# Casting the next chunk's B and C one part a step, behind a bank copy on ScalarE

## The chip, the cores and the metric

The kernel runs on one core of a Trainium2 chip. The metric is the device time of one launch in microseconds, as the median of several runs. The engines of the core are TensorE (PE, with its weight loads as PEld), VectorE (DVE), ScalarE (ACT), GpSimd (POOL) and SyncE (SP). Here SP computes nothing; it only issues the DMAs, all on one queue.

## What is computed

Three layers follow one another. The first is a linear attention (a scan with decay) over 4 batches, 8 heads and 768 positions, with head dimension 32 and state size 16. The second and third are feed-forward layers on the 3072 x 256 result. The reference computes the scan in chunks; this is the core of it:

```python
for c in range(nc):
    CB = np.einsum('bhin,bhjn->bhij', Cc, Bc)
    M = CB * L                                  # L: decay from j to i, causal
    y_intra = np.einsum('bhij,bhjd->bhid', M, xc)
    y_inter = np.einsum('bhin,bhnd->bhid', Cc, state) * decay_to_i[:, :, :, None]
    y[:, :, sl] = y_intra + y_inter
    state = decay_full * state + np.sum(Bx, axis=2)
h = np.maximum(np.maximum(x @ w1, x @ w2), x @ w3)      # layer 1, d_ff 768
x = h @ w_out
gate = 1.0 / (1.0 + np.exp(-(x @ w_gate)))              # layer 2, d_ff 1536
out = gate * (x @ w_val) @ w_out
```

## The kernel before, in words

**Attention.** The kernel cuts the 768 positions into 8 chunks of 96 (`CH`), and each chunk into 8 steps of four of the 32 (batch, head) units, so there are 64 steps. A step (`attention`, L259) computes the scores of its four units on PE (L273, from `bi` and `cs`, into the PSUM tile `s`), multiplies them by decays into `mt`, and multiplies `xs` by `mt` into the PSUM tile `y` (L291). Steps with an even number copy the scores on ACT (L281) and multiply on POOL (L282); the others do both at once on DVE (L285). After every four steps the result goes to `xt_hi` (ACT, L300) and `xt_lo` (DVE, L302), the input of layer 1.

**B and C.** From chunk 2 on, the scores need B and C as three bfloat16 parts each. `split_bc` (L231) does this for one chunk. It loads the 128 x 896 tile `bc`, then three times casts it on ACT into one third of the tile `parts` (L239) and copies that third with DMAs into `bi` and `cs` (L244); between two casts POOL subtracts the part from `bc` (L248). The first cast is followed by six copies, the second by four, the third by two. The tiles `bc` and `parts` exist once. `bi` exists twice (even and odd chunks), and so does `cs`. The generator of chunk c+1 is put into the list `pipe` by `prepare` (L311) at the first step of chunk c. Every tick of the program then takes each generator in `pipe` one stage further, however many steps are begun between two ticks. `prepare` also loads the decays of four pairs of steps ahead (`load_decay`, L206, four buffers) and scans those that have come (L228, on DVE).

**Feed-forward layers.** Layer 1 has six tiles of 512 tokens (`t`) and six blocks of 128 hidden columns (`m`); its banks are called u3_t_m_j, for j from 0 to 2. `layer` computes the three up-projections of a block into three PSUM banks. The pool of these banks, `psu`, has three buffers, and the scores tiles `s` come out of the same pool. Fp32 products are made of three matmuls of split operands (L338 to L340). `most` (L380) copies the first bank into `s3_t_m` on ACT (L383, the bank copy), takes the maximum with the other two on DVE (L385, L387), and `hidden` splits the result into `hi` (ACT, L376) and `lo` (POOL, L378), which the down-projection reads (o6 in the order, `o` in the trace). The attention of later chunks is woven into layer 1, and from token tile 2 on its steps are begun two at a time. Layer 2 begins once layer 1 is through; its weights are loaded and decoded before, when attention has ended and its memory is free.

**Order of the work.** The program's order, the pools and the waits go through a scheduler that places every instruction at a simulated time, and from that comes one fixed order for each engine. On the chip each engine works through that order and waits where a semaphore isn't there yet. `tc.issue_after(i)` adds an edge without a semaphore: what is written inside the block on the engine of `i` comes behind `i` in that engine's order.

Of the kernel before, what the change touches and what calls it, by code (L numbers as in the profile page):

```python
# [66 lines left out]
def scan_attention_then_ffn(ctx: ExitStack, tc: tile.TileContext, xh, ah, bch, pick, bn, w1, w2, w3,  # L67
                            wo1, wg, wv, wo2, out):
    nc = tc.nc
    act, dve, pool, pe, sp = nc.scalar, nc.vector, nc.gpsimd, nc.tensor, nc.sync  # L70
# [13 lines left out]
    pipe = Pipe()  # L84
# [119 lines left out]
    def load_decay(n, src):  # L204
        t = awk.tile([128, PU, LW], F32, tag="dec", bufs=DECS, name=f"dec{n}")
        i = sp.dma_start(out=t.rearrange("p u w -> p (u w)"), in_=src[n].partition_broadcast(128))  # L206
        dec[n] = t
        for _ in range(BEHIND.get(n, 0)):
            with tc.issue_after(i.ins):
                load_weights()  # L210

    def load_x(c, part=slice(0, NU)):
        if c not in xs:
            xs[c] = awk.tile([128, NU, D], F32, tag="xs", name=f"xs{c}")
            bx[c] = awk.tile([128, NU, N], F32, tag="bx", name=f"bx{c}")
        for t, src, n in ((xs[c], xh, D), (bx[c], bn, N)):
            sp.dma_start(out=t[:, part].rearrange("i u d -> i (u d)"),
                         in_=src[:, c, n * part.start:n * part.stop])

    def decay(n, clip=False):  # L220

        t = dec[n]
        if clip:
            dve.tensor_scalar(out=t[:, :, 1:LW], in0=t[:, :, 1:LW], scalar1=1e-6, scalar2=1.0,
                              op0=ALU.max, op1=ALU.min)
        for h in range(PU // 4):
            f = t[:, 4 * h:4 * h + 4].rearrange("p u w -> p (u w)")
            dve.tensor_tensor_scan(out=f, data0=f, data1=delta.rearrange("p u w -> p (u w)"),  # L228
                                   initial=0.0, op0=ALU.mult, op1=ALU.add)

    def split_bc(c):  # L231

        r = awk.tile([128, BW + 384], F32, tag="bc", bufs=1, name=f"bc{c}")
        sp.dma_start(out=r, in_=bch[:, c])
        parts = awk.tile([128, 3, BW + 384], BF16, tag="parts", bufs=1, name=f"parts{c}")
        cs[c] = awk.tile([KT, NU, CH], BF16, tag="cs", name=f"cs{c}")
        yield
        for p in range(3):
            act.copy(parts[:, p], r)  # L239
            for k, (dst, cols) in enumerate(((bi[c % 2], slice(0, BW)),  # L240
                                             (cs[c], slice(BW, BW + 384)))):
                for t, pr in enumerate(TERMS):
                    if pr[k] == p:
                        sp.dma_start(  # L244
                            out=dst[16 * t:16 * t + 16].rearrange("n (g q) i -> n g (q i)", q=4),
                            in_=parts[:, p, cols])
            if p < 2:
                pool.tensor_tensor(out=r, in0=r, in1=parts[:, p], op=ALU.subtract)  # L248
                yield

    steps = [(c, g) for c in range(NC) for g in range(NG)]
    done = [0]
    last = [None]

    def need(t):
# [3 lines left out]
    def attention(k, ahead):  # L259
# [24 lines left out]
        else:  # L284
            last[0] = dve.tensor_tensor(out=m[:, :, 0:CH], in0=ps[:, :, 0:CH], in1=dc[:, :, 1:LW],  # L285
                                        op=ALU.mult)
        prepare(k)
        yield
        y = ys[g // 4]
# [21 lines left out]
    def prepare(k):  # L311

        c, g = divmod(k, NG)
        if g == 0 and 0 < c < NC - 1:
            load_x(c + 1)
            pipe.add(split_bc(c + 1))
        n = k // 2
        if k % 2 == 0:
            if 5 <= n + 4 < NC * NP:
                load_decay(n + 4, ad)  # L320
        elif k < 9:
            decay(n + 1, n == 0)
        else:
            for i in ([n + 1] if k == 9 else []) + [n + 2]:
                if i < NC * NP:
                    with tc.issue_after(last[0].ins) if k > FIRST else ExitStack():
                        decay(i)
# [46 lines left out]
    def hidden(s, hl, eng):  # L374
        yield
        act.copy(hl[0], s)  # L376
        yield
        eng.tensor_tensor(out=hl[1], in0=s, in1=hl[0].bitcast(F32), op=ALU.subtract)  # L378

    def most(s, banks, hl):  # L380

        yield
        act.copy(s, banks[0])  # L383
        yield
        dve.tensor_tensor(out=s, in0=banks[1], in1=s, op=ALU.max)  # L385
        yield
        dve.tensor_tensor(out=s, in0=banks[2], in1=s, op=ALU.max)  # L387
        yield from hidden(s, hl, pool)
# [73 lines left out]
    for t in range(NTT):  # L462
        for m in range(M1):
            for hl in layer(t, m, wt1[m], 3, most):
                slot_end()
                slot += 1
            if pend is not None:
                down(*pend)
            slot_end()
            slot += 1  # L470
            pend = (t, m, M1, wt1[m], hl, finish1)
            if t == NTT - 1 and m == 0:
                actx.close()
                wp2.append(ctx.enter_context(tc.tile_pool(name="wp2", bufs=1)))
                todo += [(piece2, m, part) for m in range(M2) for part in range(2)]
                while todo:
                    load_weights()
            if t == NTT - 1 and m == 3:
                pipe.add(split_y(0))
# [84 lines left out]
```

## Time and profile before

| what | us |
|---|---|
| runs of the kernel before | 606.14, 601.85, 602.65 |
| median | 602.65 |
| the profiled execution | 604.28 |
| its span, first to last instruction | 602.5 |
| PE busy in it | 563.0 |
| mean granted clock of PE | 0.974 |

The profile is one execution. Times in its rows are microseconds from the start of the span unless they are marked ns. A row of instructions names the engine, the line, the operation, and the tiles as out<-in. In square brackets stands how long the engine was idle before the instruction and what ended that idle time. SPq is the DMA queue of SP. A matmul's row can overlap the next one, since matmuls are pipelined. Trace rows leave the buffer and step numbers out of tile names; the order of the instructions has them.

### The profile page before, as it was taken

The numbers are of one execution on the slowest core, as the hardware profiler recorded it, in microseconds if no ns is written. First come the engines' busy times: TensorE is split into PE (matmuls) and PEld (weight loads), VectorE is DVE, ScalarE is ACT, GpSimd is POOL, SyncE is SP. The second block draws the span as 40 slices with busy tenths as digits, with TensorE's granted clock in tenths as the row PEclk, the third lists the DMA queues.
The fourth block names the chain that finished last, engine by engine and source line by source line (L and its number), as shares of the span: only waits on it lengthen the run. The fifth ranks groups of instructions, "written<-read, shape, count | busy, mean of one in ns | idle before, by whom it ended". The sixth has DMA issues, their size and how long they took to land.

```text
span 602.5 us, 8006 instructions
## 1 busy us (share of the span) xinstructions
PE 563.0 (93%) x2992; PEld 444.7 (74%) x2992; DVE 317.5 (53%) x467; ACT 260.0 (43%) x475; POOL 186.0 (31%) x207
## 2 busy tenths in 40 slices
PE   5778797997989999999999999999999999999997
PEld 4656575675767777777768888888888888888885
DVE  4899962644745755368987133344344334334332
ACT  5777653224233223279897243233233223223322
POOL 3668874335453424237668210000000000000000
PEclk9859998998999989999999999999999999999999
DMA  7998975373763900099000000000000000000000
GB/s 252 326 313 233 205 183 93 102 132 86 155 134 83 178 28 1 1 316 312 1 2 0 2 35 1 0 1 35 2 0 36 0 1 36 1 1 35 1 0 35
DMA packets 35367, 50.53 MB, mean 84 GB/s; under 512 B 3456, under 2 KB 24320, under 8 KB 35328
## 3 DMA queue, kind: packets, MB, share of 16 engines
q1 hardware_dynamic: 35328, 50.02, 32.0%
q8 instruction: 23, 0.38, 0.3%
q14 instruction: 16, 0.13, 0.1%
HBM read 38.51 MB, written 3.25 MB: 69 GB/s over the span
## 4 chain that ended last, share of the span: by engine, by line
PE 63%; DVE 9%; DMA 8%; ACT 5%; issue 4%; POOL 2%; SPq 1%; DVEq 0%; ACTq 0%; POOLq 0%
PE u L338 14%; PE u L339 14%; PE u L340 14%; PE o L339 7%; PE o L340 6%; PE o L338 6%; DMA cs<-parts 4%; DVE dec L228 2%; DMA dec<-ad 1%; DMA bc<-in_bch 1%; DVE t_b L142 1%; DVE s L387 1%; DVE s L385 1%; PE y L291 1%; POOL lo L378 1%
## 5 line engine op out<-in xcount | busy, mean ns | idle before, releaser
L376 ACT CAST hi<-s 128x512 fp32r<-128x512 f32 x108 | 67.1, 621 | 193.1 <-DVE s L394 153.8
L394 DVE TENSOR_TENSOR s<-u,s 128x512 f32<-128x512 f32 x72 | 49.7, 690 | 126.2 <-PE u L340 125.9
L338 PE MATMUL u<-xt_hi,w_b 128*128 128x512 f32 x288 | 112.4, 390 | 0.8 <-DVE s L385 0.6
L339 PE MATMUL u<-xt_lo,w_b 128*128 128x512 f32 x288 | 112.1, 389 | 0.0
L340 PE MATMUL u<-xt_hi,w_b 128*128 128x512 f32 x288 | 112.1, 389 | 0.0
L338 PE MATMUL u<-xt_hi,w_a 128*128 128x512 f32 x216 | 90.8, 420 | 10.4 <-ACT s L383 5.8
L339 PE MATMUL u<-xt_lo,w_a 128*128 128x512 f32 x216 | 87.2, 404 | 1.8 <-DVE xt_lo L302 1.8
L340 PE MATMUL u<-xt_hi,w_a 128*128 128x512 f32 x216 | 87.0, 403 | 0.0
L378 POOL TENSOR_TENSOR lo<-s,hi 128x512 fp32r<-128x512 f32 x48 | 66.4, 1384 | 64.1 <-ACT hi L376 63.0
L338 PEld LDWEIGHTS u<-xt_hi,w_b 128*128 128x128 f32 x288 | 54.1, 188 | 13.3 <-DVE s L385 1.1
L378 DVE TENSOR_TENSOR lo<-s,hi 128x512 fp32r<-128x512 f32 x60 | 41.5, 692 | 40.6 <-ACT hi L376 40.4
L340 PEld LDWEIGHTS u<-xt_hi,w_b 128*128 128x128 f32 x288 | 54.1, 188 | 11.3
L339 PEld LDWEIGHTS u<-xt_lo,w_b 128*128 128x128 f32 x288 | 54.1, 188 | 11.0
L338 PEld LDWEIGHTS u<-xt_hi,w_a 128*128 128x128 f32 x216 | 42.2, 195 | 25.1 <-ACT s L383 8.0
L228 DVE TENSOR_TENSOR_SCAN dec<-dec,delta 128x388 f32<-128x388 f32 x64 | 57.9, 944 | 3.2 <-DMA dec<-ad 3.0
L339 PE MATMUL o<-lo,w_b 128*128 128x512 f32 x144 | 56.1, 390 | 0.0
L340 PE MATMUL o<-hi,w_b 128*128 128x512 f32 x144 | 56.0, 389 | 0.0
L339 PEld LDWEIGHTS u<-xt_lo,w_a 128*128 128x128 f32 x216 | 42.1, 195 | 10.3 <-DVE xt_lo L302 2.3
L340 PEld LDWEIGHTS u<-xt_hi,w_a 128*128 128x128 f32 x216 | 42.0, 194 | 9.5
L392 ACT ACTIVATE s<-u 128x512 f32<-128x512 f32 x72 | 43.2, 600 | 10.8 <-PE u L340 9.8
L385 DVE TENSOR_TENSOR s<-u,s 128x512 f32<-128x512 f32 x36 | 24.6, 685 | 40.4 <-PE u L340 25.8
L338 PE MATMUL o<-hi,w_b 128*128 128x512 f32 x144 | 45.3, 390 | 0.5 <-ACT hi L376 0.5
(60 smaller groups left out, 761.6 us busy)
## 6 DMA issues: line engine op xcount, KB each, us to landing
dec<-ad SPq DMA_DIRECT2D x30, 388.0 KB, 5.6
raw_a<-in_w SPq DMA_DIRECT2D x18, 256.0 KB, 6.2
bi<-parts SPq DMA_DIRECT2D x36, 128.0 KB, 6.7
cs<-parts SPq DMA_DIRECT2D x36, 96.0 KB, 6.8
xs<-in_xh SPq DMA_DIRECT2D x6, 512.0 KB, 7.1
raw_b<-in_wg SPq DMA_DIRECT2D x12, 256.0 KB, 5.8
raw_b<-in_wv SPq DMA_DIRECT2D x12, 256.0 KB, 5.8
raw_b<-in_wo SPq DMA_DIRECT2D x12, 256.0 KB, 5.8
```

What stands on the lines that cost most here:

```text
L142: dve.scalar_tensor_tensor(out=t, in0=f1, scalar=3, in1=sg, op0=ALU.logical_shift_left, op1=ALU.bitwise_or)
L228: dve.tensor_tensor_scan(out=f, data0=f, data1=delta.rearrange("p u w -> p (u w)"), initial=0.0, op0=ALU.mult, op1=ALU.add)
L291: pe.matmul(y[32 * q:32 * q + 32, g % 4, 0:CH + N], xs[c][:, 4 * g + q, :], m[:, q, :], start=True, stop=True)
L338: pe.matmul(ps, wlo, a_hi(k), start=k == 0, stop=False)
L339: pe.matmul(ps, whi, a_lo(k), start=False, stop=False)
L340: pe.matmul(ps, whi, a_hi(k), start=False, stop=k == kn - 1)
L376: act.copy(hl[0], s)
L378: eng.tensor_tensor(out=hl[1], in0=s, in1=hl[0].bitcast(F32), op=ALU.subtract)
L385: dve.tensor_tensor(out=s, in0=banks[1], in1=s, op=ALU.max)
L387: dve.tensor_tensor(out=s, in0=banks[2], in1=s, op=ALU.max)
L392: act.activation(out=s, in_=banks[0], func=AF.Sigmoid)
L394: dve.tensor_tensor(out=s, in0=banks[1], in1=s, op=ALU.mult)
```

## The change

The generator of the next chunk is kept in a list `splits` and no longer in `pipe`. `prepare`, which runs once for each of the 64 steps, takes it one stage further, so the load is issued at the first step of a chunk, and the three casts come at the second, third and fourth. From chunk 3 on each cast is also written behind the last bank copy of `most` traced so far (`evict[0]`). The generator yields `splits` itself after its third cast, and so `prepare` knows that it has ended.

```diff
@@ split_bc
         for p in range(3):
-            act.copy(parts[:, p], r)
+            with tc.issue_after(evict[0].ins) if c > 2 else ExitStack():
+                act.copy(parts[:, p], r)
...
             if p < 2:
                 pool.tensor_tensor(out=r, in0=r, in1=parts[:, p], op=ALU.subtract)
-                yield
+            yield splits if p == 2 else None
@@
     done = [0]
+    evict = [None]
+    splits = []
@@ prepare
             load_x(c + 1)
-            pipe.add(split_bc(c + 1))
+            splits.append(split_bc(c + 1))
+        if splits and next(splits[0], None) is splits:
+            splits.pop()
@@ most
-        act.copy(s, banks[0])
+        evict[0] = act.copy(s, banks[0])
```

Line numbers after the change are higher: L239 becomes L240, L244 becomes L245, L281 becomes L284, L376 becomes L381, L383 becomes L388.

The first place is ScalarE's order at the first two blocks of token tile 1 in layer 1, before. In `s3_1_0` stand the number of banks, the token tile and the block; `parts5` is chunk 5's; the last number of a name is a running one.

```order
L383 COPY s3_1_0_951<-u3_1_0_0_954 128x512
L281 COPY mt4_102<-s3_0_962 128x4x96
L239 CAST parts5_1378<-bc5_1376 128x896
L357 COPY y1_91<-o6_0_0_640 128x512
L376 CAST hi3_1_0_952<-s3_1_0_951 128x512
L357 COPY y1_91<-o6_0_1_641 128x512
L239 CAST parts5_1378<-bc5_1376 128x896
L383 COPY s3_1_1_1025<-u3_1_1_0_1028 128x512
L281 COPY mt1_99<-s3_2_1048 128x4x96
```

The same place in ScalarE's order after the change:

```order
L388 COPY s3_1_0_951<-u3_1_0_0_954 128x512
L240 CAST parts4_985<-bc4_983 128x896
L284 COPY mt4_102<-s3_0_962 128x4x96
L362 COPY y1_91<-o6_0_0_640 128x512
L362 COPY y1_91<-o6_0_1_641 128x512
L381 CAST hi3_1_0_952<-s3_1_0_951 128x512
L388 COPY s3_1_1_1025<-u3_1_1_0_1028 128x512
L240 CAST parts4_985<-bc4_983 128x896
L284 COPY mt1_99<-s3_2_1042 128x4x96
```

Chunk 5's casts have left this place and chunk 4's stand here, each directly behind a bank copy; before, chunk 4's stood ahead of these rows.

The second place is ScalarE's order at blocks 3 and 4 of token tile 2, before:

```order
L383 COPY s3_2_3_1550<-u3_2_3_0_1553 128x512
L281 COPY mt0_98<-s5_0_1569 128x4x96
L300 CAST xt_hi_92<-y1_104 128x2x2x96
L281 COPY mt2_100<-s5_2_1634 128x4x96
L376 CAST hi3_2_3_1551<-s3_2_3_1550 128x512
L239 CAST parts7_1941<-bc7_1939 128x896
L383 COPY s3_2_4_1644<-u3_2_4_0_1647 128x512
L239 CAST parts7_1941<-bc7_1939 128x896
```

The same place in ScalarE's order after the change:

```order
L388 COPY s3_2_3_1550<-u3_2_3_0_1553 128x512
L240 CAST parts6_1611<-bc6_1609 128x896
L284 COPY mt0_98<-s5_0_1569 128x4x96
L303 CAST xt_hi_92<-y1_104 128x2x2x96
L284 COPY mt2_100<-s5_2_1642 128x4x96
L381 CAST hi3_2_3_1551<-s3_2_3_1550 128x512
L388 COPY s3_2_4_1652<-u3_2_4_0_1655 128x512
L240 CAST parts6_1611<-bc6_1609 128x896
```

Where a cast of chunk 7 stood ahead of the bank copy of block 4, a cast of chunk 6 now stands behind that copy, and another behind the bank copy of block 3. Chunk 7's stand in token tile 3.

The third place is SyncE's queue where chunk 7's copies are issued, before. `dec28` is the decay load of steps 56 and 57.

```order
L206 DMA dec27_1851<-ad_105 128x776
L244 DMA bi1_97<-parts7_1941 16x8x512
L244 DMA cs7_1942<-parts7_1941 16x8x384 x3
L244 DMA bi1_97<-parts7_1941 16x8x512
L217 DMA xs7_1912<-in_xh 128x1024
L244 DMA bi1_97<-parts7_1941 16x8x512
L244 DMA cs7_1942<-parts7_1941 16x8x384 x2
L206 DMA dec28_1916<-ad_105 128x776
```

The same place in SyncE's queue after the change:

```order
L206 DMA dec27_1851<-ad_105 128x776
L245 DMA bi1_97<-parts7_1918 16x8x512 x3
L245 DMA cs7_1919<-parts7_1918 16x8x384
L217 DMA xs7_1912<-in_xh 128x1024
L245 DMA cs7_1919<-parts7_1918 16x8x384 x2
L206 DMA dec28_1920<-ad_105 128x776
```

Before, two more copies into `bi1` stand ahead of `dec27`, so `dec28` had ten copies of chunk 7 ahead of it; now it has the six of the first cast, and the four of the second come behind it.

## Rows read from the trace of the kernel before

**Rows 1.** Page, part 1: busy time, share of the span, instructions.
```profile
PE 563.0 (93%) x2992; PEld 444.7 (74%) x2992; DVE 317.5 (53%) x467; ACT 260.0 (43%) x475; POOL 186.0 (31%) x207
```

**Rows 2.** Busy time by stretches: length, PE PEld DVE ACT POOL, PE clock, DMA share, GB/s.
```profile
97.80:100.27 2.47, 0.00 (x0) 0.00 (x1) 0.00 (x0) 1.99 (x4) 0.92 (x1) 0.99 0.02 6
100.27:102.76 2.49, 1.28 (x2) 0.57 (x2) 0.00 (x0) 1.93 (x4) 2.49 (x4) 0.50 0.00 0
102.76:107.20 4.44, 4.44 (x12) 3.20 (x13) 0.69 (x1) 1.25 (x2) 2.96 (x3) 0.52 0.11 15
...
136.96:140.77 3.81, 0.00 (x1) 0.00 (x0) 0.86 (x2) 1.47 (x3) 0.46 (x1) 1.00 0.13 26
140.77:145.30 4.53, 4.53 (x14) 3.39 (x15) 0.69 (x1) 2.25 (x4) 4.44 (x4) 0.62 0.28 69
...
167.10:186.00 18.90, 15.76 (x85) 11.58 (x85) 8.81 (x16) 7.05 (x12) 9.99 (x11) 1.00 0.44 84
...
209.90:212.47 2.57, 0.87 (x21) 0.57 (x20) 2.39 (x7) 0.48 (x1) 1.18 (x2) 1.00 0.04 12
212.47:216.00 3.53, 3.53 (x9) 2.84 (x10) 2.13 (x3) 1.21 (x2) 1.53 (x2) 0.55 0.37 113
```

**Rows 3.** Waits of PE, 75 to 255 us: total us, times, longest.
```profile
PE u L338 <- ACT s L383: 5.3, 2, 3.8
PE o L338 <- ACT hi L376: 2.5, 1, 2.5
PE o L339 <- POOL lo L378: 2.5, 3, 1.2
PE s L273 <- DVE s L385: 1.2, 1, 1.2
PE u L338 <- DVE s L387: 0.9, 2, 0.5
```

**Rows 4.** Timeline of ACT: start, duration, instruction, idle time before it.
```profile
98.28 0.94 ACT L239 CAST parts<-bc 128x896 bf16<-128x896 f32 x1 [9.06 <-DMA bc<-in_bch]
...
139.30 0.94 ACT L239 CAST parts<-bc 128x896 bf16<-128x896 f32 x1 [5.43 <-DMA cs<-parts]
140.14 0.58 ACT L383 COPY s<-u 128x512 f32<-128x512 f32 x1
...
174.07 0.94 ACT L239 CAST parts<-bc 128x896 bf16<-128x896 f32 x1 [5.85 <-DMA cs<-parts]
```

**Rows 5.** Instructions on the tile parts: ns min/median/max; last, its copies' time to landing.
```profile
L244 SPq DMA_DIRECT2D cs<-parts x36: 547/597/1571, 26.7 to 200.6; - x36
L239 ACT CAST parts<-bc x18: 921/938/942, 19.1 to 180.0; 128x896 bf16<-128x896 f32 x18
L248 POOL TENSOR_TENSOR bc<-bc,parts x12: 1887/1900/2351, 20.1 to 178.0; 128x896 f32<-128x896 f32 x12
...
DMA to landing us min/median/max: 3.0/6.7/9.4
```

**Rows 6.** Line 234, the load of bc: time from issue to landing.
```profile
DMA to landing us min/median/max: 3.3/5.1/7.4
```

**Rows 7.** Timeline of all engines, 147.8 to 161.2 us.
```profile
147.86 0.59 ACT L383 COPY s<-u 128x512 f32<-128x512 f32 x1 [0.20 <-PE u L340]
...
151.05 0.69 DVE L387 TENSOR_TENSOR s<-u,s 128x512 f32<-128x512 f32 x1 [1.02 <-PE u L340]
...
151.78 0.33 SPq L217 DMA_DIRECT2D bx<-in_bn  x1
...
159.22 0.53 SPq L206 DMA_DIRECT2D dec<-ad  x1
...
160.81 0.34 PE L273 MATMUL s<-cs,bi 96*128 96x96 bf16 x4
161.01 0.59 ACT L383 COPY s<-u 128x512 f32<-128x512 f32 x1
```

**Rows 8.** Timeline of DVE at 207 us.
```profile
207.44 1.81 DVE L228 TENSOR_TENSOR_SCAN dec<-dec,delta 128x388 f32<-128x388 f32 x2 [1.22 <-DMA dec<-ad]
```

## The prediction

> **What bounds the kernel now.** I read the page's busy table first, then busy time by stretches, then the list of waits of TensorE (PE), then the timelines of the engines at its stops. PE is busy 93% of the span and no other engine reaches 60% [rows 1], so an edit on ScalarE (ACT) counts only where it lets PE stop, or where it takes such a stop away. The stretches show where PE stops between 75 and 255 us [rows 2]. It is idle for 2.47 us from 97.80, for 1.21 of the next 2.49 (busy 1.28), for 3.81 from 136.96, for 3.14 of the 18.90 from 167.10 (busy 15.76), and for 1.70 of the 2.57 from 209.90 (busy 0.87). That is 12.3 us, and the list of waits adds up to the same: 5.3 + 2.5 + 2.5 + 1.2 + 0.9 = 12.4 [rows 3].
>
> After three of these stops the matmuls also run slower. The granted clock is 0.50 and 0.52 behind the first stop, 0.62 behind the second and 0.55 behind the last; 0.50 is the 1.2 GHz level, and before each fall PE had stood still. In the stretch from 167.10, with several shorter stops, it stays at 1.00, the 2.4 GHz level [rows 2]. A busy stretch of length L at a mean clock c loses about (1 - c) x L: 0.50 x 1.28 = 0.64, 0.48 x 4.44 = 2.13, 0.38 x 4.53 = 1.72, 0.45 x 3.53 = 1.59. Idle and clock together are 18.4 us, all that can be won here.
>
> Who holds PE up? In the first three stops an instruction of ACT: its copy of a bank (L383), which frees PSUM for PE, or the cast hi (L376), which the down-projection reads [rows 3]. ACT's own timeline shows what it was doing: it sat 9.06 us before the cast at 98.28, waiting for the load bc, 5.43 before the one at 139.30 and 5.85 before the one at 174.07, both waiting for copies out of parts [rows 4]. The bank copy at 140.14 follows directly on the second [rows 4]. These are first casts of chunks 5, 6 and 7. ACT works in order, so a cast that waits for a DMA holds every bank copy behind it.
>
> **The change part by part.** Same instructions, other places: 18 casts of 0.94 us, 12 subtractions of 1.90 us on GpSimd (POOL), 72 copies on SP's queue [rows 5]. Nothing is added or removed. ScalarE's order shows the move: chunk 5's casts leave the first blocks of tile 1, chunk 4's stand there, each directly behind a bank copy, and where chunk 7's casts stood now stand chunk 6's. The casts come up to a chunk later, so their inputs have long landed.
>
> *First stop.* The 9.06 us wait goes. Chunk 4's casts, now in its place, need a load that landed long before and are separated by the subtraction of 1.90 us [rows 5], which runs while PE works on the next bank. Won: 2.47 + 1.21 + 0.64 + 2.13 = 6.45.
>
> *Second stop.* The bank copy comes before the cast instead of behind it. Won: 3.81 + 1.72 = 5.53.
>
> *Third stop.* 3.14, less 0.45 that is one of the two waits for DVE L387 [rows 3], which the casts don't cause: 2.69, no clock lost.
>
> *Last stop.* 1.24 of the 1.70 is the wait s L273 <- DVE s L385 [rows 3]. VectorE was late because its scan (L228) waited 1.22 us for a decay load [rows 8]. In SP's old order that load (dec28) stands behind ten copies of chunk 7, in the new one behind six. Four copies at 0.55 to 0.60 us of issue each [rows 5] are 2.2 to 2.4 us, more than 1.22; against it, the first cast now comes later. I take the gain, 1.24 + 1.59 = 2.83, and keep 0 as the other end. The other 0.47 us here, also a wait for L387, stays.
>
> Sum of gains: 6.45 + 5.53 + 2.69 + 2.83 = 17.5.
>
> *What the moved casts cost.* Behind a first cast stand ACT's copy of the next scores bank (L281), the casts xt_hi, and on POOL, behind the subtraction, the multiply (L282) that the next step's matmuls read. For chunks 5 and 6 these come up to 0.94 + 1.90 = 2.84 us later than if nothing stood there. The trace doesn't show that, so the bounds are 0 (PE has other matmuls to do) and 2 x 2.84 = 5.7; below nothing is excluded, because nothing leaves this path. The nearest rows are the two short waits of 0.9 us together that PE has for VectorE behind such steps [rows 3]. I take 0.8.
>
> *The new deadline.* Chunk 5's copies were ready long before they were needed; now they come late. Its second cast follows the bank copy at 147.86, and the third follows the cast hi, which waits for the maximum ending at 151.05 + 0.69 = 151.74 [rows 7]. So: hi to 152.4, cast to 153.3, two copies issued by about 154.4, the last at 153.8. From there to landing 3.0 to 9.4 us, median 6.7 [rows 5]: 156.8 to 163.2. PE wants them at 160.81 [rows 7]. The margin is +4.0 to -2.4 us. SP has few transfers in flight there (only four copies and a bx ahead), so I take the short end and cost it at 0; the other end is 2.4 plus a slow clock as in the second stop, 4.1. Chunks 4, 6 and 7 have more blocks in between. The early stage (to 75 us) only swaps a few neighbours; PE has no stop from 75.00 to 97.80 to show for it, and I count nothing.
>
> Net: 17.5 - 0.8 = 16.7. The profiled execution took 604.28 us (span 602.5 and 1.8 around it) and becomes 587.6. The median of the runs, 602.65, lies 1.6 below the profiled one, so the forecast for a median is 586.0.
>
> *A rule that speaks against it.* ACT's three long waits are for tiles that exist once (bc and parts) [rows 4]. The Trainium skill, Perfetto Trace Analysis, section Identifying Performance Opportunities, says that a gap repeating on the engine that should be saturated can mean that there isn't enough memory for the next tile, that is too few buffers. The change leaves the buffers alone, so by this rule a bubble would come back. That is the first rival; the trace so far shows the same wait at three places, which agrees with the rule, but at each the waiting cast stood early.
>
> **The rivals.** *The single buffers bite again.* Chunk 6's load may start only when chunk 5's third cast has read bc: issued at about 154.4, landing 3.3 to 7.4 us later [rows 6], 157.7 to 161.8. Chunk 6's first cast, behind the bank copy at 161.01 + 0.59 [rows 7], starts at 161.6 and also overwrites parts, whose last copy lands by 156.8 to 163.2. The margin goes from +3.9 to -1.6. If it is missed, ACT stands again and holds the next scores copy; priced like the second stop, 5.5 us: 591.5. For it: both tiles are single. Against: the bounds are mostly on the safe side.
>
> *SP holds the last copies, and it gets slower.* SP issues in order, and chunk 5's last copies stand behind a bx load that waits for a buffer. In the trace it went at 151.78; if it slipped to the next release, at 159.22 [rows 7], the last copy would go at about 160.4 and land at up to 169.8. PE, also in order, would stand 9.0 us at the first scores of chunk 5, plus 1.7 of clock: 10.7. The same at chunk 6, and its first cast is held as well (5.5): 26.9 in all, 586.0 + 26.9 = 612.9. It turns slower than before once these three places lose more than 16.7 together. For it: the margin is a few us. Against: that load waits for a POOL multiply which the new order hardly delays.
>
> *It doesn't do what it says.* If the three waits were only the last of several reasons, PE would stop a little later for something else: 602.65. Against: at each stop the next bank copy or cast hi ran as soon as ACT was free.
>
> **How the numbers follow.** Forecast 0.64, with its own range 583.5 to 589.5 (below: all 18.4 won, 584.3, less the 0.8 by which the lowest run lies under the median; above: the last stop staying, 588.8, and some 0.7 more at the moved casts). Single buffers 0.22, from there to 596. No change 0.07. SP's hold 0.07. A measurement of this kernel tells about 1% (6 us) from no change; faster than 596.6 holds the first two, 0.86, within 1% the third, 0.07, slower the fourth, 0.07. The range 582.5 to 596 leaves out the last two and little more; its low end has 1 us for the early stage, which I counted at nothing.
>
> **What would show it.** Right: ACT's waits for bc and for the copies are gone from the list, PE idles under 3 us between 75 and 240, the clock stays at 1.00 there, and the stretch after layer 2 begins keeps its length. Wrong: a wait of PE for the DMA into bi or cs at the first scores of chunk 5, ACT waiting again at chunk 6's first cast, or the scan still waiting for a decay load.

## The result and the profile after

The changed kernel takes 587.79 us (median of 4 runs, 587.59 to 587.85), the kernel before beside it on the same chip 604.39 us (4 runs, 601.85 to 606.48). The ratio is 0.9727 with a 95% interval of 0.968 to 0.9773. The profiled execution's span is 585.8 us, 16.7 less than before; PE's mean granted clock is 0.997, before 0.974. These two spans are one execution each. With more runs on one chip, further down, the medians lie 14.7 us apart (602.21 to 587.47), so the profile of before is a somewhat long one.

PE's busy time after is that of [rows 1] within 1 us, as a share of a shorter span (page, part 1):

```profile
PE 564.0 (96%) x2992; PEld 448.2 (77%) x2992; DVE 317.3 (54%) x467; ACT 260.9 (45%) x475; POOL 186.9 (32%) x207
```

The waits of PE from 75 to 255 us after the change, which answer to [rows 3] (total us, times, longest):

```profile
PE s L276 <- DVE s L390: 1.2, 2, 0.9
PE u L343 <- DVE s L392: 0.4, 1, 0.4
```

12.4 us have become 1.6, and PE's granted clock is 1.00 over the stretch. No wait for ACT or POOL is left; all three are for VectorE. The longest, 0.95 us at 76.06, lies in token tile 0. It was there before as well (1.02 us at 73.19, just outside the window of [rows 3]), so behind it 0.29 and 0.44 us remain. Of ACT's own waits from 80 to 240 us, one line concerns the casts:

```profile
ACT parts L240 <- POOL bc L249: 2.1, 2, 1.8
```

The waits for DMAs of [rows 4], 20.3 us in three, are gone. What remains is the subtraction on POOL between two casts. The casts themselves run as in [rows 5] (median 941 ns, subtraction 1904 ns). The timeline of ACT shows those of chunk 5 and the first of chunk 6, none with idle time ahead of it:

```profile
130.89 0.94 ACT L240 CAST parts<-bc 128x896 bf16<-128x896 f32 x1
...
138.81 0.94 ACT L240 CAST parts<-bc 128x896 bf16<-128x896 f32 x1
...
142.35 0.94 ACT L240 CAST parts<-bc 128x896 bf16<-128x896 f32 x1
...
152.65 0.94 ACT L240 CAST parts<-bc 128x896 bf16<-128x896 f32 x1
```

To see where the time went, I cut both executions at the starts of the same bank copies (the copy into s3_t_m). Busy time by those stretches, before (columns as in [rows 2]):

```profile
41.43:88.25 46.82, 41.32 (x290) 30.68 (x289) 43.82 (x64) 31.72 (x56) 37.81 (x36) 0.99 0.93 220
88.25:102.11 13.86, 10.83 (x64) 7.26 (x60) 3.57 (x5) 4.24 (x8) 4.96 (x5) 0.93 0.71 134
102.11:129.74 27.63, 26.98 (x157) 19.06 (x158) 15.59 (x27) 7.80 (x15) 12.30 (x16) 0.91 0.39 91
129.74:147.86 18.12, 14.31 (x81) 10.93 (x80) 6.50 (x10) 6.86 (x11) 8.04 (x8) 0.91 0.54 96
147.86:161.01 13.15, 13.15 (x100) 9.99 (x98) 9.75 (x16) 3.62 (x8) 5.19 (x9) 1.00 0.60 151
161.01:174.91 13.90, 12.64 (x106) 9.24 (x102) 7.45 (x13) 3.29 (x7) 5.48 (x8) 1.00 0.99 193
174.91:191.48 16.57, 14.70 (x87) 11.14 (x88) 9.60 (x17) 7.61 (x14) 9.57 (x10) 1.00 0.14 42
...
204.61:221.98 17.37, 15.66 (x113) 11.99 (x110) 10.64 (x20) 4.03 (x9) 7.04 (x10) 0.90 0.36 87
```

The same stretches after the change:

```profile
43.48:92.20 48.72, 43.86 (x294) 32.03 (x292) 44.53 (x64) 29.37 (x52) 34.24 (x34) 0.96 0.82 194
92.20:98.22 6.02, 6.02 (x36) 4.56 (x37) 2.34 (x4) 3.52 (x7) 4.27 (x4) 1.00 0.56 85
98.22:125.87 27.65, 27.65 (x185) 19.64 (x185) 16.14 (x27) 8.67 (x16) 12.25 (x17) 1.00 0.58 120
125.87:138.32 12.45, 12.45 (x81) 9.89 (x80) 7.39 (x13) 5.20 (x10) 6.92 (x8) 1.00 0.54 94
138.32:152.18 13.86, 13.86 (x119) 10.51 (x118) 9.24 (x16) 5.24 (x10) 7.20 (x10) 1.00 0.94 214
152.18:159.69 7.51, 7.22 (x53) 5.48 (x52) 7.02 (x13) 3.29 (x8) 6.25 (x8) 1.00 0.90 170
159.69:178.34 18.65, 18.65 (x121) 14.65 (x120) 10.04 (x18) 7.62 (x14) 8.88 (x11) 1.00 0.61 138
...
191.47:205.93 14.46, 14.02 (x113) 10.75 (x110) 10.55 (x20) 4.04 (x10) 7.08 (x10) 1.00 0.56 111
```

A lesson in reading them: the count of matmuls in brackets tells whether two stretches hold the same work. In the first three rows they don't, one by one (a mark lies on ACT, and PE has done more or less by then). Nor can the rows be added, since a matmul that lasts over a mark is counted on both sides. One stretch over all three holds 506 matmuls in both executions. The fourth row has 81 in both, the next three add up to 293 in both, the last has 113 in both. So the account is made over these sums:

| stretch, by bank copies | before | after | difference |
|---|---|---|---|
| start to s3_0_0 | 41.43 | 43.48 | +2.05 |
| s3_0_0 to s3_1_5 | 88.31 | 82.39 | -5.92 |
| s3_1_5 to s3_2_1 | 18.12 | 12.45 | -5.67 |
| s3_2_1 to s3_3_1 | 43.62 | 40.02 | -3.60 |
| s3_3_1 to s3_3_3 | 13.13 | 13.13 | 0 |
| s3_3_3 to s3_3_5 | 17.37 | 14.46 | -2.91 |
| s3_3_5 to s3_4_5 | 41.05 | 40.36 | -0.69 |
| s3_4_5 to the end | 339.47 | 339.51 | +0.04 |
| span | 602.5 | 585.8 | -16.70 |

PE's idle time in a row is its length less its busy time. In the stretches from 92.20 to 205.93 it is 0.29 and 0.44 us in two rows and nothing in the others, at a clock of 1.00.

The new deadline, chunk 5's last copies, is read from SP's queue and PE's timeline:

```profile
142.35 0.53 SPq L217 DMA_DIRECT2D bx<-in_bn  x1
143.31 0.55 SPq L245 DMA_DIRECT2D bi<-parts  x1
143.91 0.59 SPq L245 DMA_DIRECT2D cs<-parts  x1
144.56 0.58 SPq L234 DMA_DIRECT2D bc<-in_bch  x1
...
151.25 0.34 PE L276 MATMUL s<-cs,bi 96*128 96x96 bf16 x4
```

The last copy's record in the trace lands at 148.65, 4.7 us after its issue. PE wants it at 151.25, so 2.6 us are left. The load of bc for chunk 6 lands at 149.61, 3.0 us before the cast at 152.65 that reads it. The bx load ahead of the copies wasn't held.

The last stop is left with the short wait alone; VectorE's scan that waited in [rows 8] has no idle time ahead of it now:

```profile
192.99 1.80 DVE L228 TENSOR_TENSOR_SCAN dec<-dec,delta 128x388 f32<-128x388 f32 x2
...
198.01 0.50 PE L343 MATMUL u<-xt_hi,w_a 128*128 128x512 f32 x1 [0.44 <-DVE s L392]
...
199.28 0.39 PE L345 MATMUL u<-xt_hi,w_a 128*128 128x512 f32 x1
199.51 0.39 PE L343 MATMUL u<-xt_hi,w_a 128*128 128x512 f32 x1
```

### The profile page after: what moved, and what is told of

The parts are those of the page before. It is cut to its first block, busy times and chain, and to the rows that moved or that the text cites. A ratio compares the mean times of both kernels' runs of the same rounds, so it can differ in the third digit from the quotient of the medians.

```text
span 585.8 us, 8007 instructions
## 1 busy us (share of the span) xinstructions
PE 564.0 (96%) x2992; PEld 448.2 (77%) x2992; DVE 317.3 (54%) x467; ACT 260.9 (45%) x475; POOL 186.9 (32%) x207
## 4 chain that ended last, share of the span: by engine, by line
PE 79%; DMA 8%; DVE 5%; ACT 3%; issue 2%; SPq 2%; DVEq 0%; ACTq 0%
PE u L343 17%; PE u L344 16%; PE u L345 16%; PE o L344 8%; PE o L343 7%; PE o L345 7%; PE s L273 3%; PE y L294 3%; DMA raw_a<-in_w 3%; PE s L276 1%; DMA dec<-in_ah 1%; DMA cs<-parts 1%; DMA raw_a<-in_wo 1%; DMA raw_b<-in_wo 1%; DVE t_b L142 1%
## 5 line engine op out<-in xcount | busy, mean ns | idle before, releaser
L381 ACT CAST hi<-s 128x512 fp32r<-128x512 f32 x108 | 67.2, 622 | 201.3 <-DVE s L399 153.7
L343 PE MATMUL u<-xt_hi,w_a 128*128 128x512 f32 x216 | 89.6, 415 | 3.9 <-DVE s L392 2.0
L383 POOL TENSOR_TENSOR lo<-s,hi 128x512 fp32r<-128x512 f32 x48 | 65.9, 1373 | 69.6 <-ACT hi L381 67.9
L344 PE MATMUL u<-xt_lo,w_a 128*128 128x512 f32 x216 | 85.9, 398 | 0.1
L345 PE MATMUL u<-xt_hi,w_a 128*128 128x512 f32 x216 | 85.4, 395 | 0.0
L383 DVE TENSOR_TENSOR lo<-s,hi 128x512 fp32r<-128x512 f32 x60 | 41.5, 692 | 40.6 <-ACT hi L381 40.5
L343 PEld LDWEIGHTS u<-xt_hi,w_a 128*128 128x128 f32 x216 | 41.3, 191 | 16.9 <-DVE s L392 2.5
L345 PEld LDWEIGHTS u<-xt_hi,w_a 128*128 128x128 f32 x216 | 41.3, 191 | 9.3
L390 DVE TENSOR_TENSOR s<-u,s 128x512 f32<-128x512 f32 x36 | 24.7, 685 | 19.6 <-PE u L345 16.7
```

The source lines that it names most:

```text
L343: pe.matmul(ps, wlo, a_hi(k), start=k == 0, stop=False)
L344: pe.matmul(ps, whi, a_lo(k), start=False, stop=False)
L345: pe.matmul(ps, whi, a_hi(k), start=False, stop=k == kn - 1)
```

## The experiments

The theory from the prediction: a cast that waits for a DMA, ahead of a bank copy in ACT's order, holds up the bank copy and with it PE; the edge behind the bank copy ends that. The rivals: the pace of one cast a step does it; the single buffers do it (and would bring the stops back); nothing of it decides. The first four runs had the kernel before beside them at 601.96 us (17 runs, 599.24 to 606.03), the other four at 602.21 us (16 runs, 597.5 to 606.33).

### One a step, without the edge

```diff
-            with tc.issue_after(evict[0].ins) if c > 2 else ExitStack():
-                act.copy(parts[:, p], r)
+            act.copy(parts[:, p], r)
```

> One half of the change: the casts come one a step, but are not queued behind a bank copy. The scheduler is free to place them as early as their inputs allow. Theory A (the edge behind the bank copy does the work, the pace by itself doesn't): chunk 5's casts stand directly behind chunk 4's as before, ScalarE waits over 5 us three times for the load or the copies, and the time is that of before, 600 to 606 us. Theory B (spreading the casts over steps is enough): ScalarE's long waits are gone, and the time is 588 to 592.

Measured: 603.95 us (10 runs), ratio 1.0047 [1.0016, 1.0078]. Its waits of PE (75 to 255 us), then of ACT at the casts (80 to 240 us):

```profile
PE u L342 <- ACT s L387: 7.2, 3, 3.6
PE s L275 <- DVE s L389: 2.4, 1, 2.4
...
ACT parts L239 <- DMA cs<-parts: 11.4, 2, 6.2
ACT parts L239 <- DMA bc<-in_bch: 8.1, 2, 5.1
```

What was taken away is only the edge; the pace stays. The scheduler then puts the casts where they were before, ACT waits 19.5 us for DMAs at them, and PE waits 7.2 us for the bank copy again. The pace alone wins nothing.

### The edge, without the pace

```diff
 # the kernel before, with the edge alone
-            act.copy(parts[:, p], r)
+            with tc.issue_after(evict[0].ins) if c > 2 else ExitStack():
+                act.copy(parts[:, p], r)
...
-        act.copy(s, banks[0])
+        evict[0] = act.copy(s, banks[0])
```

> The other half: the old list, one stage at every tick, but from chunk 3 on each cast is queued behind the last bank copy. Theory A (the edge does the work): no ScalarE wait for the load or the copies over 2 us, PE idle under 4 us between 75 and 240, time 586 to 591. Theory B (it needs the pace too, since without it a cast still comes too early by a block): one or two of the three stops come back, time 593 to 600.

Measured: 586.56 us (4 runs, 585.65 to 587.74), ratio 0.9743 [0.9707, 0.9778]. The generator stays in `pipe` here. All that ACT waits for at its casts from 80 to 240 us:

```profile
ACT parts L240 <- POOL bc L249: 0.3, 1, 0.3
```

This is the whole gain of the change. Together with the run above: the edge is sufficient, and without it there is none. But the edge does two things at once. It puts the cast behind the bank copy, and it puts it much later: chunk 5's first cast starts at 131.01 us here and at 98.28 before [rows 4], and finds nothing left to wait for. No run separates the two, say with a cast as late but ahead of the bank copy.

### The kernel before with two buffers

```diff
-        r = awk.tile([128, BW + 384], F32, tag="bc", bufs=1, name=f"bc{c}")
+        r = awk.tile([128, BW + 384], F32, tag="bc", bufs=2, name=f"bc{c}")
-        parts = awk.tile([128, 3, BW + 384], BF16, tag="parts", bufs=1, name=f"parts{c}")
+        parts = awk.tile([128, 3, BW + 384], BF16, tag="parts", bufs=2, name=f"parts{c}")
```

> The kernel before, with two buffers for bc and for parts and nothing else. Buffer theory (the stops come from tiles that exist once; the rule of the Trainium skill, Perfetto Trace Analysis, section Identifying Performance Opportunities): ScalarE's waits for DMAs at the casts go, the stops near 98, 137 and 167 us go, and the time is 587 to 589, with the last stop for dec28 left. Order theory (a cast stands ahead of a bank copy whose input comes later): the wait moves to the next resource, the load bc itself or the copies into bi, which still exist twice; 593 to 600, with at least 3 us of ScalarE waiting for a DMA left at the casts.

Measured: 602.29 us (10 runs), ratio 0.9995 [0.996, 1.0029]. Both theories' times were missed, the buffer theory's by 13 us or more. ACT's timeline at two first casts, then PE's:

```profile
102.56 0.94 ACT L239 CAST parts<-bc 128x896 bf16<-128x896 f32 x1 [6.10 <-DMA bc<-in_bch]
...
143.75 0.94 ACT L239 CAST parts<-bc 128x896 bf16<-128x896 f32 x1 [4.89 <-DMA cs<-parts]
144.59 0.58 ACT L383 COPY s<-u 128x512 f32<-128x512 f32 x1
...
103.93 0.33 PE L273 MATMUL s<-cs,bi 96*128 96x96 bf16 x4 [2.82 <-ACT mt L281]
...
145.22 0.51 PE L338 MATMUL u<-xt_hi,w_a 128*128 128x512 f32 x1 [3.27 <-ACT s L383]
```

ACT still waits 11.0 us at the casts of chunks 6 and 7. With a second buffer the scheduler places casts earlier, so chunk 6's first cast waits for the copies of chunk 4 and chunk 7's for those of chunk 5. SP issues those late, in order behind others that wait. The waits of its queue from 76 to 150 us show the longest for such a copy, 7.4 us until PE's scores of the older chunk have read `bi`, which still exists twice:

```profile
SPq L244 <- PE s L273: 7.4, 1, 7.4
```

(The first row of ACT names the load; but in the trace the last copy of chunk 4 lands at 102.31, 0.25 us ahead of the cast, and the only load then under way is chunk 7's, at 103.16.) Only the stop near 175 us is gone. From the bank copy of s3_1_0 to that of s3_5_5 this kernel takes 201.26 us, before 210.00 and the changed one 189.31. So two buffers win 8.7 us there. Most of it is lost earlier: its first bank copy starts at 44.69 us, and from there to s3_1_0 it takes 51.18 us where before took 46.82. Casts of chunks 4 and 5 now stand among token tile 0's blocks; that they cause this loss was not tried by itself, and neither were two buffers without it.

The rule weighed in the prediction (the Trainium skill, Perfetto Trace Analysis, section Identifying Performance Opportunities: a repeating bubble can mean too few buffers) agrees with one of the three stops, the one near 175 us, which goes. Two stops of 2.82 and 3.27 us of idle PE stay with two buffers, and the time stays at 602.29; another order with the same buffers gives 586.56.

### Chunk 7 as before

```diff
-            with tc.issue_after(evict[0].ins) if c > 2 else ExitStack():
+            with tc.issue_after(evict[0].ins) if 2 < c < 7 else ExitStack():
...
-            splits.append(split_bc(c + 1))
+            if c == 6:
+                pipe.add(split_bc(c + 1))
+            else:
+                splits.append(split_bc(c + 1))
```

> The changed kernel with chunk 7 alone cast and copied as before: old list, no edge. Theory A (the last stop came from the decay load of steps 56 and 57 standing behind ten copies of chunk 7, and the third from chunk 7's first cast waiting ahead of a bank copy): VectorE's scan waits about 1 us for that load, PE loses 2.8 us there with its slow clock, and a stop of about 1 us comes at the cast, which waits for a load and copies that land some 71 us before the end of attention's weave; together 590 to 592 us. Theory B (these copies are not what delays the load): within 1 us of the changed kernel, 587 to 589.

Measured: 594.42 us (4 runs, 591.6 to 595.97), ratio 0.9867 [0.9826, 0.9907]; the profiled execution is the lowest, 591.6. ACT and PE at the third stop, VectorE and PE at the last, and the stretches around them:

```profile
170.43 0.94 ACT L240 CAST parts<-bc 128x896 bf16<-128x896 f32 x1 [5.50 <-DMA bc<-in_bch]
...
171.94 0.96 PE L346 MATMUL o<-hi,w_a 128*128 128x512 f32 x2 [1.84 <-ACT hi L384]
...
196.62 1.81 DVE L228 TENSOR_TENSOR_SCAN dec<-dec,delta 128x388 f32<-128x388 f32 x2 [1.00 <-DMA dec<-ad]
...
200.86 0.33 PE L276 MATMUL s<-cs,bi 96*128 96x96 bf16 x4 [1.01 <-DVE s L393]
...
171.94:176.00 4.06, 4.06 (x11) 3.15 (x12) 0.95 (x2) 1.75 (x3) 4.06 (x5) 0.58 0.00 0
...
202.20:206.00 3.80, 3.80 (x18) 3.13 (x17) 2.28 (x3) 0.70 (x2) 1.54 (x2) 1.00 0.41 107
```

Only chunk 7's casts differ from the changed kernel, and with them both late stops come back. At the third, ACT waits 5.50 us for the load, PE 1.84 us for cast hi, and the clock falls to 0.58. At the last, the scan waits 1.00 us for its decay load again and PE 1.01 us for VectorE, as in [rows 8]; in SP's queue ten copies of chunk 7 stand ahead of dec28 again. So that stop comes with those copies. Between the bank copies of s3_2_5 and s3_3_1 this costs 3.7 us against the changed kernel, between those of s3_3_3 and s3_3_5 1.1 us (the medians lie further apart, 6.6 us from 587.79, and the 594.42 lies above the 590 to 592 that was expected; what makes up the rest stays open).

### Chunk 5's third cast later

```diff
         for p in range(3):
+            for _ in range(4 if (c, p) == (5, 2) else 0):
+                yield
             with tc.issue_after(evict[0].ins) if c > 2 else ExitStack():
```

> The changed kernel with chunk 5's third cast alone four steps later, which puts it one block of layer 1 further down, behind the next bank copy. The measured margin at chunk 5's first scores was 2.6 us (last copy landed 148.65, scores at 151.25). If that margin is all there is, the cast moves some 3 to 4 us, the last copy lands at about 152, PE waits 0 to 1 us for the DMA at the first scores of chunk 5, and the time is 587.5 to 589. Rival: the copies take SP's queue past a held bx or decay load and PE waits several us at a slow clock, 592 or more. If no wait appears and the time is as the changed kernel's, the margin is larger than read.

Measured: 587.49 us (4 runs, 585.92 to 587.98), ratio 0.9743 [0.9704, 0.9782]. SP's queue and PE at the first scores of chunk 5:

```profile
145.47 0.56 SPq L247 DMA_DIRECT2D bi<-parts  x1
146.08 0.59 SPq L247 DMA_DIRECT2D cs<-parts  x1
146.72 0.58 SPq L234 DMA_DIRECT2D bc<-in_bch  x1
...
151.06 0.52 PE L278 MATMUL s<-cs,bi 96*128 96x96 bf16 x8
```

From the bank copy of s3_2_1 (138.32 in the changed kernel, 137.41 here) the third cast comes 7.09 us later where it came 4.03: 3.06 us later. The last copy lands at 150.16 and PE wants it at 151.06. No wait appears and the time doesn't change, but 0.9 us is all that is left of the margin. (PE's order also shifted: the scores come 13.65 us after that bank copy, in the changed kernel 12.93.) So the margin fell as the trace let one expect once PE's 0.7 us and a landing 0.7 us quicker are counted, and the wait of 0 to 1 us that was expected didn't come. What a missed deadline costs was not measured: one step later still, the copies would stand behind the scores that read them in the program.

### Chunk 2 through the old list, and the changed kernel again

```diff
-            splits.append(split_bc(c + 1))
+            if c == 1:
+                pipe.add(split_bc(c + 1))
+            else:
+                splits.append(split_bc(c + 1))
```

> The changed kernel, but chunk 2 alone goes through the old list again, so that the order of the first stage, up to the first blocks of layer 1, is that of before. In the changed kernel's profile the bank copy of block 4 of token tile 0 comes at 79.03 us, 2.87 later than before. Theory A (the change costs this: chunk 2's copies now stand ahead of a decay load and two weight loads): that copy comes at about 76.2 again, and the time falls by 2 to 4 us, to about 585. Theory B (the first stage differs between executions of any kernel, with the DMA queue full): the copy comes anywhere between 76 and 79, and the time stays at 587.8.

Measured: 586.54 us (6 runs, 584.47 to 587.89), ratio 0.9741 [0.9711, 0.9772], between the times of the two theories. Its first bank copy starts at 41.61 us, like that of before, and the changed kernel's at 43.48. To tell the order from chance, both were run on one chip:

> The changed kernel once more, beside the run with chunk 2 through the old list. Chunk-2 theory (chunk 2's three casts at one a step put decay and x copies of the early stage about 1 us later): this run is about 1 us slower than the other, some 587.5 against 586.5, and from the first bank copy of layer 1 to the third it needs about 0.8 us more. Rival, the early stage of an execution simply falls into one of two states (first bank copy at about 41.6 or at about 43.3 us) whatever the kernel: the two runs are within 0.4 us of each other once the first bank copy falls at the same time.

> The changed kernel, but with chunk 2 in the old list; chunks 3 to 7 as changed. Chunk-2 theory: about 586.5, 1 us faster than the changed kernel on the same chip. Rival: within 0.4 us of it. In either case both early states (first bank copy near 41.6 or near 43.3 us) can occur.

Measured: the changed kernel 587.47 us (6 runs, 585.34 to 589.15), ratio 0.9749 [0.9713, 0.9785]; with chunk 2 in the old list 586.76 us (6 runs, 584.68 to 586.95), ratio 0.9728 [0.9696, 0.976]. The first bank copy starts at 41.02 and at 41.31 us, so the 43.48 is not the order's doing. From s3_0_0 to s3_1_5 the changed kernel takes 82.39 and 82.34 us in its two profiles, the other 81.39 and 83.50: its own two differ by more than it does from the changed one. From the first bank copy to the third, where 0.8 us were expected, the two differ by 0.3 (19.75 and 19.41). The sign named for the run before, the bank copy of block 4, came at 76.61 us there, but at 76.55 in the changed kernel's second profile and at 78.05 with chunk 2 in the old list, so it doesn't tell the two kernels apart. The 0.7 us between the medians lies inside the scatter of the runs; whether chunk 2's pace costs up to 1 us stays open.

## Why the prediction was right

The time came out 1.8 us above the forecast of 586.0, inside the range and inside the likeliest case's own range. The 1.8 come from the last step of the forecast, which put the median 1.6 us below the profiled execution, as before; after the change it lies 0.2 above it. The profiled execution came out at 587.59, where 587.6 was put, and its span 16.7 us shorter, as the sum had it. But that the sum hit so closely is luck: errors in it cancelled, and the medians of more runs lie only 14.7 us apart. By the account over the bank copies:

- *First stop* with token tile 0, from s3_0_0 on, counted at nothing: 5.92 won where 6.45 was put. All of the stop is gone. Two parts hide in it. From s3_1_0 to s3_1_5 the time falls from 41.49 to 33.67 us, with four matmuls fewer; at 0.23 us each that leaves about 6.9 won by the stop. From s3_0_0 to s3_1_0 it grows from 46.82 to 48.72 with four more, so about 1.0 was lost there. Whether the change costs that is open: the four profiles of the changed kernel and of the one with chunk 2 in the old list take 47.73 to 49.83 there, and those of one kernel differ by 2.1.
- *Second stop*: 5.67, put at 5.53.
- *Third stop* less *what the moved casts cost*: 3.60, put at 2.69 - 0.8 = 1.89. This was mis-sized, in two ways. No cost of the moved casts shows here, where 0.8 was put: PE has other matmuls while POOL subtracts, and its waits for VectorE grew no longer (0.29 us in all, before 0.45). And a stop costs more than its idle time. PE's idle time in the stretch went from 3.13 to 0.29 us, 2.84 less, but its busy time fell too, from 40.49 to 39.73 for the same 293 matmuls. A 128x512 matmul's row lasts 0.39 us while they start every 0.23, so each loses its overlap with the next, 0.16 us, where PE stops; by this estimate four waits make 0.6 of the 0.76. The 0.45 that I left out as VectorE's own went with the rest, and 0.29 of another wait came.
- *Last stop*: 2.91, put at 2.83. Four copies less ahead of dec28 were enough; with chunk 7 as before, the scan waits again. That kernel lost only 1.1 us here, though, because the clock didn't fall.
- *The new deadline*: 0, as put. The margin was worked out as +4.0 to -2.4 us and measured at 2.6; the copies landed after 4.7 us, on the short side of 3.0 to 9.4, as assumed. That the few transfers in flight are the reason isn't shown.
- *Early stage*: counted at nothing, and 2.05 us were lost before the first bank copy. The same kernel's other profile starts that copy at 41.02, so the loss is that execution's and no cost of the change. It cancelled the 1.7 by which the third stop and the moved casts were put too low. The 0.69 between s3_3_5 and s3_4_5 are three matmuls at 0.23: PE is busy throughout, and the stretch holds 253 of them after and 256 before (255 and 0.33 us less in the second profile of the same kernel). Why the bank copy comes three matmuls earlier is not known.

Of the rivals, *the single buffers* didn't bite: no wait came back with them (bc landed 3.0 us ahead of chunk 6's first cast). Doubling them left the time of the kernel before where it was, though one of its stops went. *SP's hold* didn't occur, since the bx load went on time. *It doesn't do what it says* fell with the list of PE's waits. One thing the prediction didn't separate: it priced the pace and the edge as one. The runs show that the edge alone does it; what they leave open is whether the cast's place behind the bank copy or its later time matters more.

## What to carry to other kernels

When an engine that works in order frees the resource of the busiest engine, look at what its long waits hold up behind them, not only at what they wait for. Here an edge that put an instruction whose DMA was late behind the copy that the busiest engine was waiting for took the waits away; a second buffer alone let the scheduler place it still earlier, and two of three waits stayed. After such a move, work out the margin to the next deadline from issue times and measured landings: here 2.6 us were enough, and 0.9 still were.

## What was not expected of the hardware

In these runs, how much clock a stop costs can't be read from its length, and what decides it stays open. Before, PE stood for 1.24 + 0.47 us at the last stop and the granted clock fell to 0.55; with chunk 7 as before it stood for 1.01 + 0.47 at the same place and the clock stayed at 1.00. With two buffers a stop of 2.82 us was followed by 1.00, and one of 3.27 us by 0.67:

```profile
104.00:109.00 5.00, 3.90 (x34) 2.45 (x34) 2.28 (x3) 2.99 (x5) 4.84 (x4) 1.00 0.22 78
...
145.22:149.00 3.78, 3.77 (x11) 3.02 (x12) 0.69 (x1) 2.25 (x4) 3.78 (x4) 0.67 0.09 32
```

And one program's beginning varies: the first bank copy of layer 1 started at 41.0 and at 43.5 us in two profiles of the changed kernel, in a stretch whose mean DMA share is 0.92 and 0.91.
